# Attention and expert kernel on one core: k's second half prepared in round 0, q's copies behind round 0, the first pair's later loads behind round 4

## The chip, the cores and the metric

One core of a Trainium2 chip runs the program. The metric is the device time of one execution in microseconds (us). The engines have short names: PE is TensorE (matrix products and transposes), DVE is VectorE, ACT is ScalarE, POOL is GpSimd, and SP is SyncE, which here only issues transfers and passes semaphores. SPq in a row is SP's instruction queue. PEld is the weight load that belongs to a product on PE.

## The reference

Attention over pooled queries, whose output feeds four experts, weighted by the gate:

```python
q_pool = q.reshape(B, H, S // 2, 2, D).mean(axis=3)      # B=2, H=8, S=1152, D=64
scores = scale * np.matmul(q_pool, k.transpose(0, 1, 3, 2))
attn = np.exp(scores - np.max(scores, axis=-1, keepdims=True))
attn = attn / (np.sum(attn, axis=-1, keepdims=True) + 1e-09)
x = np.matmul(attn, v)  # then transposed to [B*S/2, H*D] = [1152, 512]
for e in range(4):
    h = np.maximum(x @ w1[e], 0.0)                       # w1[e]: [512, 1024]
    out += p[:, e:e + 1] * (h @ w2[e])                   # w2[e]: [1024, 512]
```

Everything is float32. The kernel writes each operand as a high part and a low part and adds three products of them.

## The kernel before

The attention comes first, then the experts. The change touches the attention alone. Heads are taken two at a time: eight pairs, `n` = 0 to 7, nine score tiles of 128 pooled queries by 1152 keys in each pair.

The loop over `n` runs five **rounds**, `round_(n, 0)` to `round_(n, 4)`. A round transposes two finished tiles (round 3: one), which is line 207 on PE with operand `sx`, makes the scores of tiles three places ahead (lines 384 and 392), and adds a part of the product with v (`PV_part`, line 478). DVE takes the minima of the scores (`neg_scores`, 444), ACT the exponentials (450), and both copy transposes out of PSUM (340, 342). The scores run ahead, so that round 4 of pair n already makes the scores of pair n+1. At its end a round may prepare **items**: `item_q` and `item_k` transpose pieces of the coming pair's q and k on PE, ACT copies them to `raw`, and POOL splits them into a high and a low part (`pool_split`, 214 and 215). `KTS` gives three pieces of k: 0 is key tile 8 and travels with `item_q`, 1 is tiles 0 to 3, and 2 is tiles 4 to 7, k's second half.

POOL's results still lie in the wrong rows. `stack_k` (285) copies k from `kab` to `k2` on chip, two transfers of 64 rows. `move_q` (293) copies a half `y` of q from the staging area `stq` to `q2`, two transfers; a pair needs four. `load_q` (170) and `load_kv` (174) fetch from memory. All of these are issued by SP, in program order.

One more thing stands in SP's queue. From pair 1 on, the scores of two tiles share a PSUM bank, and `S_rows` orders them by a **relay**: SP's `nop` at line 402 waits for a product on PE (tile f+1's columns), and PE's first product of tile f's last 128 columns waits for the relay:

```python
mm = [S_term(s, t2, 1, j) for j in range(3)][-1]
relay = nc.sync.nop()
tc.add_manual_dep(relay.ins, mm.ins.name, SYNC, reason="row tiles of one bank")
```

There is one relay in each of the rounds 0, 1, 2 and 4. What SP has in front of a relay must be issued before the relay can pass; and a transfer that waits, or that takes long to issue, holds the relay and PE behind it.

Of the kernel before, what the change touches and what calls it, by code (L numbers as in the profile page):

```python
# [17 lines left out]
def attention_moe_kernel(ctx, tc, q, k, v, probs, w1, w2, out):  # L18
    nc = tc.nc
# [3 lines left out]
    P = 128  # L23
# [23 lines left out]
    xr = const.tile([P, NKT, NT], F32, name="xr")  # L47
# [6 lines left out]
    kn = kq[:, :2 * KT * D].rearrange("p (h t d) -> p h t d", h=2, t=KT)  # L54
# [44 lines left out]
    WCH = [(0, 2), (2, 4), (4, 6), (6, 7)]  # L99
# [48 lines left out]
    with ExitStack() as actx:  # L148
# [18 lines left out]
        def load_q(n, t0=0, t1=9):  # L167
            b, hp = pairs[n]
            src = q[b, 2 * hp:2 * hp + 2].rearrange("h (p t r) d -> (h p) t r d", p=HALF, t=9)
            nc.sync.dma_start(qn[:, t0:t1], src[:, t0:t1])  # L170

        def load_kv(dst, src, n, h0=0, h1=2):
            b, hp = pairs[n]
            nc.sync.dma_start(
                dst[:, h0:h1], src[b, 2 * hp + h0:2 * hp + h1].rearrange("h (p t) d -> p h t d", p=P))
# [106 lines left out]
        def stack_k(n, t0, t1):  # L282
            cols = slice(t0 * P, t1 * P)
            for h in range(2):
                nc.sync.dma_start(  # L285
                    k2[n % 2][ROWS[1 - h], :, cols].bitcast(F32), kab[n % 2][ROWS[h], :, cols].bitcast(F32))

        def move_q(n, y):
            for half in range(2):
                r = slice(half * HALF, (half + 1) * HALF)  # L290
                dst = q2[n % 2].rearrange("p z s (y x) -> p (z s) y x", y=2)[r, :, y, :]
                st = stq.rearrange("p z s j x -> p (z s) (j x)")[y * HALF:(y + 1) * HALF]
                nc.sync.dma_start(dst.bitcast(F32), st.bitcast(F32))  # L293
# [33 lines left out]
        def item_r(n, grp, eng):  # L327
            r = rs[n % 2][:, 4 * grp:]

            def use(pt):  # L330
                copy(eng, halves(rb[grp], 0, 2), pt[:, :, :2])
                if grp:
                    for a, h in enumerate(ROWS):
                        copy(eng, rb[1][h, 256:], pt[h, a, 2])
            return [spread[:, j * P:(j + 1) * P] for j in range(2)] + (
                [r[:, 4:5].to_broadcast([P, P])] if grp else []), use
# [145 lines left out]
        def inv_sums(n, grp):  # L482
            c0, c1 = ((0, 4), (4, 9))[grp]
            r = rs[n % 2][:, c0:c1]
            nc.vector.tensor_scalar_add(r, sums[n % 2][:, c0:c1], 1e-9)
            nc.vector.reciprocal(r, r)
            nc.vector.tensor_copy(
                spread.rearrange("p (c x) -> p c x", x=HALF), r[:, :4].unsqueeze(2).to_broadcast([P, 4, HALF]))
# [113 lines left out]
        def load_probs():  # L602
            for hh in range(2):
                nc.sync.dma_start(
                    pr.rearrange("p (b t) e -> p b t e", b=2)[hh * HALF:(hh + 1) * HALF],
                    probs.rearrange("(b p t) e -> p b t e", b=2, p=HALF))

        def gate_weights():
            nc.vector.tensor_reduce(prs, pr, AX.X, ALU.add)
            nc.vector.tensor_scalar_add(prs, prs, 1e-9)  # L610
            nc.vector.reciprocal(prs, prs)
            nc.gpsimd.tensor_tensor(pr, pr, prs.unsqueeze(2).to_broadcast([P, 18, E]), ALU.mult)
            for a in range(2):
                sl = slice(a * HALF, (a + 1) * HALF)
                nc.gpsimd.tensor_copy(pw[sl], pr[sl, a:a + 17:2, :])
# [5 lines left out]
        def round_(n, r, items=(), spare=(), beside=(), wide=False, before=None, mid=None, ahead=False, heads=both, swap=True):  # L621
            ts_ = [g for g in ((9 * n + 5,) if r == 3 else [9 * n + (-1, 1, 3, 0, 6)[r] + j for j in range(2)]) if g >= 0]
            x, count, side = ts_[0], len(ts_), first[0]
            f = x + 3
            transposed([(x, 0, 8)], tp, heads)
            if before:
                before()
            rest = scores(f, count, side, wide)
            transposed([(x, 8, 9)] + [(g, 0, 1) for g in ts_[1:]], tp, both[:1], beside)
            for g in pending:  # L630
                exps(g)
            pending.clear()
            neg_scores(f)

            def prepared():
                if spare:
                    prepare(spare, tp)
                if items:
                    prepare(items, SIDE[side if count == 2 else 1 - side])

            if count == 2:
                scores2(f + 1, rest)
                transposed([(ts_[1], 1, 9)], tp, both)
                exps(f)
                if ahead:
                    prepared()
                neg_scores(f + 1)
            pending.append(f + count - 1)
            if mid:
                mid()  # L650
            pn, grp, k0, k1 = ((n - 1, 1, 0, 5), (n - 1, 1, 5, 9), (n, 0, 0, 3), (n, 0, 3, 6), (n, 0, 6, 9))[r]
            if pn >= 0:
                PV_part(pn, grp, k0, k1)
                if k1 == KT:
                    finish(pn, grp)
            if not ahead:
                prepared()
            if items and count == 2 and swap:
                first[0] = 1 - side
            while behind:  # L660
                behind.pop(0)()

        for n in range(NP):
            last = n == NP - 1
            two = n + 2 < NP

            if n == 0:
                round_(0, 0, [item_k(1, 1, nc.scalar), item_k(1, 2, nc.scalar)], wide=True)
            elif n == 1:
                round_(1, 0, [item_r(0, 1, nc.vector), item_k(2, 1, nc.scalar)], [item_k(2, 2, nc.scalar)],  # L670
                       before=lambda: inv_sums(0, 1))
            else:
                round_(n, 0, [item_r(n - 1, 1, nc.vector)], before=lambda: inv_sums(n - 1, 1))
            if n and two:
                load_q(n + 2)
                load_kv(kn, k, n + 2)
            if n > 1 and not last:
                move_q(n + 1, 0)
            if last:
                split_x("S3", 1, slice(0, HT), xr[:, 1, :HT], nc.gpsimd)  # L680
                load_w2(0)
                w1_hi(0, WCH[:1])
                w1_lo(0, WCH[:1])


            if n == 0:
                round_(0, 1, [item_q(1, nc.vector)], wide=True, before=lambda: add_q(nc.vector), ahead=True, swap=False)
                load_q(2)
                load_kv(kn, k, 2)
                load_kv(vn[1], v, 1)  # L690
                load_probs()
            elif n == 1:
                round_(1, 1, [item_q(2, nc.scalar)])
                stack_k(2, 0, 9)
            elif last:
                round_(n, 1)
                w1_hi(0, WCH[1:2])
                w1_lo(0, WCH[1:2])
            else:
                round_(n, 1, [item_k(n + 1, 2, nc.scalar)])  # L700
                stack_k(n + 1, 0, 9)
                move_q(n + 1, 1)


            round_(n, 2, [item_r(n, 0, nc.vector)], before=lambda: inv_sums(n, 0),
                   heads=both if n else both[:1] * 2, swap=n > 0)
            if n == 0:
                split_q2m(1, rawq(1))
            if n == 1:
                move_q(2, 0)  # L710
                move_q(2, 1)
            if n and two:
                add_q(nc.gpsimd)
                join_k(0)
                join_k(1)
            if n == NP - 2:
                load_w1(0)
            if last:
                w1_hi(0, WCH[2:])
                w1_lo(0, WCH[2:])  # L720
                load_w1(1)


            round_(n, 3, [item_q(n + 2, nc.scalar)] if n and two else [])
            if n and not last:
                load_kv(vn[(n + 1) % 2], v, n + 1)
            if n == 0:
                add_q(nc.gpsimd)
                join_k(0)
                join_k(1)  # L730
                join_k(2, xr[:, 1, :4 * P])
            if last:
                break


            round_(n, 4, [item_k(n + 2, 1, nc.scalar)] if n and two else [])
            if n == 1:
                gate_weights()
            if n == NP - 2:
                w1_sums(0)  # L740
# [188 lines left out]
```

## Time and profile before

| | |
|---|---|
| median of 3 runs | 679.97 us (678.71 to 680.31) |
| the profiled execution's own time | 681.35 us |
| its span, first to last instruction | 679.5 us |
| mean granted clock of TensorE | 0.952 |
| PE busy in the span | 624.0 us (92%) |
| DVE, ACT, POOL busy | 381.9, 297.4, 340.0 us |

The span is the time between the first and the last instruction of the profiled execution; 1.85 us of its own time lie around it. Attention takes the first 300 us or so. In rows of a timeline the columns are: start in us, duration in us, engine, line, operation, what is written from what, sizes, and how many instructions are merged; in square brackets stands how long the engine had been idle, and what ended that.

### The profile page before, as it was taken

Reading aid. Unit: us, or ns where it says so; the run is one execution under the profiler, and the core shown is the slowest. Engines: PE = TensorE matmul, PEld = TensorE weight load, DVE = VectorE, ACT = ScalarE, POOL = GpSimd, SP = SyncE. Lnnn points to the kernel's source line nnn. Section 1 sums busy time; section 2 is a strip of 40 time slices with the busy share of each in tenths; the row PEclk is TensorE's granted clock in tenths of the full one; section 3 lists DMA queues with packets and bytes.
Section 4 is the critical chain, followed back from the end, with each engine's and each line's share of the span. In section 5 each row is a group of like instructions: output and inputs, shape, how many; then the busy total and the mean of one; then the engine's idle time right before and its main releaser. Section 6 shows DMA issues by size and latency. Waiting matters only on the chain.

```text
span 679.5 us, 12422 instructions
## 1 busy us (share of the span) xinstructions
PE 624.0 (92%) x5045; PEld 523.8 (77%) x5045; DVE 381.9 (56%) x583; ACT 297.4 (44%) x545; POOL 340.0 (50%) x392
## 2 busy tenths in 40 slices
PE   8897959596887959979999999999999999999997
PEld 7665747384665747749889989988998899899886
DVE  6855747566583838666454445445444544544454
ACT  5754736364564727726244234423422441343130
POOL 4435434334142315857685467447645854674240
PEclk9987988989796969979999999999999999999999
DMA  4964652625445160111121111112120210210005
GB/s 149 211 194 90 161 121 59 143 72 139 98 111 127 34 167 32 33 31 42 53 63 32 40 53 49 46 32 62 32 63 32 62 32 32 62 34 28 32 1 139
DMA packets 38584, 50.90 MB, mean 75 GB/s; under 512 B 3072, under 2 KB 27008, under 8 KB 37632
## 3 DMA queue, kind: packets, MB, share of 16 engines
q1 hardware_dynamic: 37648, 48.94, 27.5%
q10 hardware_dynamic: 880, 1.18, 0.5%
q8 instruction: 39, 0.64, 0.4%
q14 instruction: 17, 0.14, 0.1%
HBM read 30.97 MB, written 2.36 MB: 49 GB/s over the span
## 4 chain that ended last, share of the span: by engine, by line
PE 86%; SPq 5%; DVE 3%; POOL 3%; issue 1%; ACT 1%; DMA 1%; DVEq 0%; ACTq 0%; POOLq 0%
PE banks L885 29%; PE banks L137 26%; PE banks L478 11%; PE banks L207 8%; PE banks L392 8%; SPq L293 3%; PE banks L384 3%; POOL kk L215 1%; SPq L285 1%; DMA kq<-in_k_dram 1%; DVE sx L444 1%; ACT raw L340 1%; POOL kk L214 1%; DVE q2all L546 0%; DVE aT L342 0%
## 5 line engine op out<-in xcount | busy, mean ns | idle before, releaser
L885 PE MATMUL banks<-w2s,hb 128*128 128x512 f32 (+1 forms) x876 | 199.3, 387 | 0.0
L885 PEld LDWEIGHTS banks<-w2s,hb 128*128 128x128 f32 x876 | 162.5, 188 | 32.7
L889 DVE SCALAR_TENSOR_TENSOR acc<-banks,pw,acc 128x512 f32<-128x512 f32 (+1 forms) x137 | 101.8, 743 | 81.0 <-PE banks L885 80.9
L444 DVE TENSOR_SCALAR_CACHE_REDUCE sx<-banks 128x1152 f32<-128x1152 f32 x72 | 97.3, 1351 | 63.4 <-PE banks L207 61.6
L118 POOL TENSOR_TENSOR kk<-kq,kk 128x512 fp32r<-128x512 f32 x64 | 72.2, 1160 | 116.1 <-ACT kk L110 116.1
L392 PE MATMUL banks<-kk,q2all 64*128 64x512 f32 (+1 forms) x504 | 75.9, 400 | 42.4 <-SPq L402 41.1
L340 ACT ACTIVATE aT<-banks 128x128 f32<-128x128 f32 (+1 forms) x145 | 59.9, 437 | 107.2 <-PE banks L207 106.2
L392 PEld LDWEIGHTS banks<-kk,q2all 64*128 64x128 f32 x504 | 56.4, 203 | 47.8 <-SPq L402 44.1
L450 ACT ACTIVATE sx<-sx,mn 128x1152 f32<-128x1152 f32 x72 | 90.4, 1256 | 2.5 <-DVE sx L444 2.5
L478 PE MATMUL banks<-aT,vn 128*64 128x320 f32 (+1 forms) x576 | 87.0, 446 | 0.0
L805 POOL TENSOR_TENSOR hb<-xr,hb 128x576 fp32r<-128x576 f32 x48 | 68.9, 1441 | 21.3 <-ACT hb L804 21.3
L137 PE MATMUL banks<-xb,kk 128*128 128x288 f32 x480 | 77.6, 298 | 0.0
L207 PE MATMUL banks<-ident,sx 64*128 64x64 f32 x1296 | 75.1, 238 | 1.0 <-ACT aT L340 0.5
L137 PE MATMUL banks<-q2all,kk 128*128 128x288 f32 x448 | 75.1, 296 | 0.0
L852 ACT ACTIVATE xr<-banks 128x576 f32<-128x576 f32 x14 | 9.1, 650 | 147.4 <-PE banks L137 147.4
L207 PEld LDWEIGHTS banks<-ident,sx 64*128 64x128 f32 x1296 | 61.2, 148 | 12.3 <-ACT aT L340 6.5
L137 PEld LDWEIGHTS banks<-xb,kk 128*128 128x128 f32 x480 | 69.0, 190 | 1.2 <-issue 1.0
L137 PEld LDWEIGHTS banks<-q2all,kk 128*128 128x128 f32 x448 | 64.6, 188 | 0.0
L478 PEld LDWEIGHTS banks<-aT,vn 128*64 128x64 f32 x576 | 40.8, 148 | 27.4 <-issue 5.3
L342 DVE COPY aT<-banks 128x512 f32<-128x512 f32 x71 | 48.9, 689 | 23.2 <-PE banks L207 22.6
L801 DVE TENSOR_TENSOR xr<-banks,xr 128x576 f32<-128x576 f32 x48 | 36.4, 758 | 40.4 <-PE banks L137 40.1
L137 PE MATMUL banks<-xa,kk 128*128 128x288 f32 x384 | 56.7, 296 | 0.0
(108 smaller groups left out, 636.8 us busy)
## 6 DMA issues: line engine op xcount, KB each, us to landing
kq<-in_moe_w_dram SPq DMA_DIRECT2D x64, 128.0 KB, 2.4
qsf<-in_moe_w_dram SPq DMA_DIRECT2D x16, 512.0 KB, 3.5
kk<-kk SPq DMA_DIRECT2D x14, 576.0 KB, 6.0
q2all<-q2all SPq DMA_DIRECT2D x28, 256.0 KB, 7.8
vn<-in_v_dram SPq DMA_DIRECT2D x8, 576.0 KB, 6.2
kq<-in_k_dram SPq DMA_DIRECT2D x7, 576.0 KB, 6.4
kq<-in_q_dram SPq DMA_DIRECT2D x7, 576.0 KB, 4.1
kk<-kk SPq DMA_DIRECT2D x4, 288.0 KB, 7.0
```

The lines of the kernel that those rows point to most:

```text
L118: nc.gpsimd.tensor_tensor(flat(w1s[u % 2][:, 1, a:b]), flat(wf[:, a:b]), flat(w1s[u % 2][:, 0, a:b].bitcast(F32)), ALU.subtract)
L137: nc.tensor.matmul(chain[:, c, :CW], w1s[u % 2][:, a, WI[wo], kt, :], xop(xo, z, kt)[:, c * CW:(c + 1) * CW], start=(first and kt == 0 and ...
L207: nc.tensor.transpose(pt[:, a, j, :], src[r], ident[r, r])
L340: nc.scalar.activation(dst, src, AF.Copy)
L342: nc.vector.tensor_copy(dst, src)
L392: return nc.tensor.matmul(dst, q2[n % 2][ROWS[a], zq, h, t * P:(t + 1) * P], src[n % 2][ROWS[a], zk, cs], start=(j == 0), stop=(j == 2), s ...
L444: nc.vector.tensor_scalar(sx[g % 3].rearrange("p (c x) -> p c x", c=c), view, -INV, None, ALU.mult, ALU.min, accum_out=mn[g % 3])
L450: nc.scalar.activation(sx[g % 3], sx[g % 3], AF.Exp, bias=mn[g % 3], scale=-1.0, accum_out=sums[n % 2][:, i:i + 1])
L478: nc.tensor.matmul(po[h * HALF:(h + 1) * HALF, :w], vn[n % 2][:, h, kt, :], aT[grp][:, h, kt, :], start=(kt == 0), stop=(kt == KT - 1))
L805: nc.gpsimd.tensor_tensor(lo, c, hi.bitcast(F32), ALU.subtract)
L885: nc.tensor.matmul(pc, h[:, a, sl, ts_], w[:, b, sl, c0:c1], start=(m == 0), stop=(m == len(ops) - 1))
L889: nc.vector.scalar_tensor_tensor(ac, pc, pw[:, tt, e:e + 1], ac, ALU.mult, ALU.add)
```

## The change

In pairs 2 to 6, `item_k(n + 1, 2)` moves from round 1 into round 0, all four copies of `move_q` stand directly behind round 0 and ahead of the loads, and `stack_k` stays behind round 1 alone. In pair 1 `stack_k` is cut in two: key tiles 0 to 7 behind round 1, and tile 8, which comes with `item_q`, behind round 2. In pair 0 the loads of pair 2's q and k, of pair 1's v and of the gate, with POOL's work on them, move from behind rounds 1 and 3 into round 4, behind its second set of scores and so behind its relay. No arithmetic is added or removed; two small transfers are added by the cut.

```diff
+        def later_loads():
+            load_q(2)
+            load_kv(kn, k, 2)
+            load_kv(vn[1], v, 1)
+            load_probs()
+            add_q(nc.gpsimd)
+            join_k(0)
+            join_k(1)
+            join_k(2, xr[:, 1, :4 * P])
...
-                round_(n, 0, [item_r(n - 1, 1, nc.vector)], before=lambda: inv_sums(n - 1, 1))
+                round_(n, 0, [item_r(n - 1, 1, nc.vector)] + ([] if last else [item_k(n + 1, 2, nc.scalar)]),
+                       before=lambda: inv_sums(n - 1, 1))
+                if not last:
+                    move_q(n + 1, 0)
+                    move_q(n + 1, 1)
             if n and two:
                 load_q(n + 2)
                 load_kv(kn, k, n + 2)
-            if n > 1 and not last:
-                move_q(n + 1, 0)
...
-                load_q(2)
-                load_kv(kn, k, 2)
-                load_kv(vn[1], v, 1)
-                load_probs()
-            elif n == 1:
-                round_(1, 1, [item_q(2, nc.scalar)])
-                stack_k(2, 0, 9)
-            elif last:
-                round_(n, 1)
-                w1_hi(0, WCH[1:2])
-                w1_lo(0, WCH[1:2])
             else:
-                round_(n, 1, [item_k(n + 1, 2, nc.scalar)])
-                stack_k(n + 1, 0, 9)
-                move_q(n + 1, 1)
+                round_(n, 1, [item_q(2, nc.scalar)] if n == 1 else [])
+                if last:
+                    w1_hi(0, WCH[1:2])
+                    w1_lo(0, WCH[1:2])
+                else:
+                    stack_k(n + 1, 0, 9 if n > 1 else 8)
...
             if n == 1:
+                stack_k(2, 8, 9)
                 move_q(2, 0)
                 move_q(2, 1)
...
-            if n == 0:
-                add_q(nc.gpsimd)
-                join_k(0)
-                join_k(1)
-                join_k(2, xr[:, 1, :4 * P])
...
-            round_(n, 4, [item_k(n + 2, 1, nc.scalar)] if n and two else [])
+            round_(n, 4, [item_k(n + 2, 1, nc.scalar)] if n and two else [], mid=None if n else later_loads)
```

In SP's queue, from pair 1's `stack_k` to pair 2's loads and copies, the transfers stand as follows (+ now, - before; the relays are no transfers and have no rows: in pair 2, one stands ahead of the first loads or copies, one ahead of `stack_k`, and one ahead of the load of v):

```order
-L285 DMA kk_74<-kk_74 64x2304 x2
+L285 DMA kk_74<-kk_74 64x2x1024 x2
+L285 DMA kk_74<-kk_74 64x2x128 x2
 L293 DMA q2all<-q2all 64x4x256 x4
 L174 DMA vn_84<-in_v_dram 128x2x576
+L293 DMA q2all<-q2all 64x4x256 x4
 L170 DMA kq<-in_q_dram 128x1152
 L174 DMA kq<-in_k_dram 128x2x576
-L293 DMA q2all<-q2all 64x4x256 x2
 L285 DMA kk_75<-kk_75 64x2304 x2
-L293 DMA q2all<-q2all 64x4x256 x2
 L174 DMA vn_85<-in_v_dram 128x2x576
```

Pair 1's stack became four transfers, and in pair 2 (as in 3 to 6) two copies of q left the place behind the stack and all four stand ahead of the loads.

On PE, the transposes of k's second half (operand `qsf`) in pair 2 stand behind round 0's items instead of behind round 1's product with v:

```order
 L207 MATMUL banks<-ident,spread 128x64 x4
 L207 MATMUL banks<-ident,rs_101 128x64 x2
+L207 MATMUL banks<-ident,qsf 128x64 x8
 L207 MATMUL banks<-ident,sx_87 128x64 x16
 L392 MATMUL banks<-kk_74,q2all 128x512 x3
```

```order
 L207 MATMUL banks<-ident,sx_88 128x64 x16
 L478 MATMUL banks<-aT_90,vn_85 64x320 x8
-L207 MATMUL banks<-ident,qsf 128x64 x8
 L207 MATMUL banks<-ident,sx_86 128x64 x16
 L392 MATMUL banks<-kk_74,q2all 128x512 x3
```

Eight transposes moved one round ahead, and nothing else changed its place on PE.

## Rows read from the trace of the kernel before

**Rows 1.** The waits by pair of engines: us in total, times, longest us

```profile
PE banks L392 <- SPq L402: 41.1, 7, 7.3
```

**Rows 2.** The timeline of SP in pair 3

```profile
116.18 0.35 SPq L170 DMA_DIRECT2D kq<-in_q_dram  x1
116.63 0.37 SPq L174 DMA_DIRECT2D kq<-in_k_dram  x1
117.06 1.26 SPq L293 DMA_DIRECT2D q2all<-q2all  x2
129.90 1.47 SPq L285 DMA_DIRECT2D kk<-kk  x2
131.43 4.46 SPq L293 DMA_DIRECT2D q2all<-q2all  x2
```

**Rows 3.** The timeline of PE in pair 3, and the start of pair 4

```profile
121.54 1.40 PE L392 MATMUL banks<-kk,q2all 64*128 64x512 f32 x12
...
127.43 1.28 PE L392 MATMUL banks<-kk,q2all 64*128 64x512 f32 x9
136.00 0.47 PE L392 MATMUL banks<-kk,q2all 64*128 64x128 f32 x1 [7.29 <-SPq L402]
...
145.20 0.53 PE L207 MATMUL banks<-ident,qsf 64*128 64x64 f32 x10
...
145.63 0.66 PE L207 MATMUL banks<-ident,sx 64*128 64x64 f32 x16
...
150.28 0.46 PE L207 MATMUL banks<-ident,qsf 64*128 64x64 f32 x8
150.58 0.66 PE L207 MATMUL banks<-ident,sx 64*128 64x64 f32 x16
```

**Rows 4.** The timeline of POOL in pair 3

```profile
128.61 1.26 POOL L215 TENSOR_TENSOR kk<-raw,kk 128x512 fp32r<-128x512 f32 x1
...
131.24 1.26 POOL L185 TENSOR_TENSOR qsf<-kq 128x512 f32<-128x512 f32 x1
```

**Rows 5.** Stretches: busy us of engines (instructions), granted clock, DMA share, GB/s

```profile
116.18:152.01 35.83, 28.54 (x357) 21.43 (x354) 23.12 (x40) 19.89 (x40) 12.86 (x21) 0.90 0.47 114
...
124.00:125.00 1.00, 1.00 (x20) 0.68 (x18) 1.00 (x3) 1.00 (x3) 0.00 (x0) 1.00 0.12 26
...
133.00:134.00 1.00, 0.00 (x0) 0.00 (x0) 0.00 (x0) 0.00 (x0) 0.94 (x3) 0.50 0.81 147
```

**Rows 6.** The timeline of PE in pair 7, which prepares no later pair

```profile
260.87 0.71 PE L207 MATMUL banks<-ident,sx 64*128 64x64 f32 x16
...
272.84 0.71 PE L207 MATMUL banks<-ident,sx 64*128 64x64 f32 x16
...
279.40 1.95 PE L384 MATMUL banks<-kk,q2all 128*128 128x512 f32 x9 [0.56 <-DVE sx L444]
...
282.94 0.71 PE L207 MATMUL banks<-ident,sx 64*128 64x64 f32 x16
```

**Rows 7.** The timeline of PE in pair 1, and the start of pair 2

```profile
41.80 0.71 PE L207 MATMUL banks<-ident,sx 64*128 64x64 f32 x16
...
55.12 0.66 PE L207 MATMUL banks<-ident,sx 64*128 64x64 f32 x16
...
61.12 0.47 PE L392 MATMUL banks<-kk,q2all 64*128 64x128 f32 x1 [4.25 <-SPq L402]
...
77.16 0.66 PE L207 MATMUL banks<-ident,sx 64*128 64x64 f32 x16
```

**Rows 8.** The timeline of SP in pairs 0 and 1

```profile
32.32 0.83 SPq L170 DMA_DIRECT2D kq<-in_q_dram  x1
33.19 1.47 SPq L174 DMA_DIRECT2D kq<-in_k_dram  x1
...
61.13 7.12 SPq L293 DMA_DIRECT2D q2all<-q2all  x4
```

**Rows 9.** The timeline of PE in round 4 of pair 0

```profile
37.00 0.32 PE L392 MATMUL banks<-kk,q2all 64*128 64x128 f32 x1 [0.35 <-SPq L402]
```

**Rows 10.** Transfers, the page's last part: count, KB each, median us to landing

```profile
q2all<-q2all SPq DMA_DIRECT2D x28, 256.0 KB, 7.8
```

## The prediction

> **What bounds the kernel now.** I read the page first: PE is busy 92% of the span, so what can be gained is the time in which PE waits, or runs at the lower clock. The list of waits says where. One row of it has 41.1 us, seven times: PE's products of line 392 wait for SP's relay [rows 1]. No other wait of PE in that list is near it in size. Seven times is once for each of the pairs 0 to 6.
>
> Then the timelines of one pair. In pair 3 PE issues the nine products that don't need the relay at 127.43, ends them at 128.71, and goes on at 136.00 after 7.29 us of nothing [rows 3]. SP's queue shows why the relay is late. POOL ends the low part of k's second half at 129.87 [rows 4]; only then does SP issue the stack, at 129.90, for 1.47 us, and behind it two copies of q that take 4.46 us to issue, until 135.89 [rows 2]. The relay of round 2 stands behind these. So the wait is POOL's lateness (128.7 to 129.9), then 1.5, then 4.5 us of issuing. The second cost is the clock: at 133 us the granted clock is 0.50, the lower level of 1.2 GHz, after PE had been idle since 128.7 [rows 5], and PE goes on at that level.
>
> The same two copies of q cost 1.26 us when they are issued behind loads and not behind a stack [rows 2]. So a copy takes long to issue where copies on the chip are still under way in front of it.
>
> **The change, part by part.** I sum against the profiled execution (681.35 us, span 679.5). Its rounds are dated by the 16 transposes that open each.
>
> *Pairs 2 to 6, the wait and the clock.* Pair 2 opens at 77.16 [rows 7] and pair 7 at 260.87 [rows 6]: 183.71 us for five pairs, 36.7 each. What would a pair take whose round 2 does not wait? Pair 7 shows it: it prepares nothing, has no transfer that waits ahead of its relays, and needs 282.94 - 260.87 = 22.07 us for rounds 0 to 3 [rows 6]. To this come round 4 with its eight transposes of k, 150.58 - 145.63 = 4.95 us [rows 3]; `item_q`'s twelve transposes in round 3, 145.63 - 145.20 = 0.43 us [rows 3]; and the eight of k's second half, now in round 0, 150.58 - 150.28 = 0.30 us [rows 3]. That is 27.75 us. Pair 6 has neither `item_q` nor the piece of k in round 4, 0.73 us less, 27.0. Five pairs: 4 x 27.75 + 27.0 = 138.0 us, a gain of 45.7 us. It splits into 5 x 7.3 = 36.5 us of waits [rows 1] and 9.2 us, 1.8 a pair, of clock. Pair 7's 0.56 us in which PE waits for DVE [rows 6] is kept in: DVE then has no pause any more in which to catch up. If it stays hidden, 2.8 us more are gained.
>
> *The moved item.* Its instructions are the same eight transposes, one copy on ACT and two splits on POOL. PE pays 0.30 us in round 0 and saves it in round 1. POOL is busy 12.86 us of 35.83 [rows 5] and has nothing else at that place, so its split ends well before round 1 does. It is late only if ACT is; ACT has 19.89 us of work in the pair [rows 5].
>
> *SP ahead of round 1's relay.* This is the new risk. Four copies and two loads now stand between the relay of round 0 and that of round 1. In pair 3 SP was free at 116.18 [rows 2]. The relay of round 1 is wanted when its nine products end: 121.54 + 1.28 = 122.82 [rows 3], plus 0.30 for the moved transposes, 123.1. So SP has 6.9 us. Cheapest, from rows: 2 x 1.26 + 0.35 + 0.37 = 3.2 us [rows 2], no wait. Dearest: four copies behind a stack took 7.12 us and two loads behind copies 0.83 + 1.47 us [rows 8], 9.4 us, a wait of 2.5 us. The copies now start with an empty queue, so at least the first two cost 0.63 us each. I take 0.5 us for each of the pairs 2 to 5 (pair 6 has no loads), 2.0 us; with the clock's 1.8 us on top, the dear end is 4 x 4.3 = 17 us.
>
> The Trainium skill, "DMA: Bandwidth & Descriptors", section "Issuing engines are not separate DMA queues", says that the time a sequencer takes to start a transfer is usually small beside the transfer itself. The trace agrees for copies behind loads and disagrees for copies behind a stack [rows 2]; by the page this term would be nothing and the time 2 us lower.
>
> *The stack behind round 1.* It no longer waits for POOL. Issued near 124, it has 5 us until round 2's relay. In the trace the loads and two copies issued from 116.18 on are off the queues in the stretch from 124 to 125, where the DMA share is 0.12 [rows 5]; with two copies more that is 127 or so, so that the stack may be held, but ends before the relay is wanted near 129. I take nothing; if it is held by the 4.5 us of [rows 2], round 2 waits for about 1 us.
>
> *The loads, 3 to 6 us later.* POOL wants the new q at 131.24 today [rows 4], some 7 us after the DMAs went quiet. Now the loads end near 127 and POOL is free for them near 129. Hidden; without that cover `item_q` of round 3, some 7 us behind, is the next to be late.
>
> *Pair 1.* It takes 77.16 - 41.80 = 35.36 us, with 4.25 us of wait and the low clock behind that [rows 7]. Now: rounds 0 and 1 as they are, 55.12 - 41.80 = 13.32 [rows 7]; rounds 2 and 3 as in pair 7, 282.94 - 272.84 = 10.10 [rows 6]; 0.43 and 4.95 as above: 28.80 us. But the four copies of q now follow only after POOL's last split, near 60, and the scores of round 4 want them near 66. They take 1.26 to 7.12 us to issue [rows 2, 8] and 7.8 us to land in the middle [rows 10], so PE waits between 0 and 5 us; I take 1.5 (the large stack is gone from in front of them). Gain: 5.1 us.
>
> *Pair 0.* The relay of round 4 waited 0.35 us [rows 9], behind loads that now come later. With some of the low clock behind it I take 1.0 us, between 0 and 2.
>
> The sum: 45.7 - 2.0 + 5.1 + 1.0 = 49.8 us. The profiled execution would take 631.6 us. The median lies 1.4 us under the profiled execution: 679.97 - 49.8 = 630.2, so 630.
>
> **The rivals.** *A, the forecast*, 630 us: nothing of size takes the place of round 2's relay. For it speaks pair 7, which runs all of its relays without a wait. *B, round 1's relay takes over*: the copies are slow even with an empty queue, and SP reaches the relay 2.5 us late, with the clock falling again. That gives back 17 - 2 = 15 us: 645. For it: 256 KB copies on chip were slow four times in a row [rows 8]. Against it: there a stack was ahead of them. *C, DVE becomes the bound*: it has 23.12 us of work per pair [rows 5], 83% of 27.75 us, and it has today a pause of 7 us in each pair. If the chain through DVE makes a pair 30 us, 2.3 us in five pairs: 641. Against it: pair 7 loses 0.56 us to DVE and no more. *D, slower*: if each copy were taken only when the one before had landed, four would hold SP for 4 x 7.8 = 31 us [rows 10]; round 1's relay would then be some 25 us late, a loss of 25 - 9.1 = 16 us a pair and 64 in four pairs, 694 us or above. It decides from 9.1 us of lateness, that is from 16 us of issuing. Two copies in 1.26 us [rows 2] speak against it. *E, the split does not come sooner*: ACT or POOL reach the moved item only a round later, and the stack waits as before. Then only the copies' 4.5 us are gone, with half the clock: 5 x 5 + 5 = 30 us, 650. POOL's idle time in that place speaks against it.
>
> **How the numbers follow.** A 0.62, B 0.17, C 0.12, E 0.06, D 0.03. The range goes from A's good end (no wait in round 1, none in pair 1, DVE hidden: 630 - 2 - 1.5 - 2.8 - 1: about 622) to B, with pair 1's dear end of 3.5 us (near 649): 622 to 649. About 0.3% is what a measurement of this kernel can tell from no change. A, B, C and E are all faster, 0.97, of which I keep 0.02 for no change and 0.01 more for slower, since several of them together eat most of the gain: 0.94, 0.02, 0.04.
>
> **What would show it.** The wait of line 392 for line 402 falls from 41 us to a few; pairs 2 to 6 open 27 to 28.5 us apart; the granted clock stays at 1.00 through rounds 2 and 3; the stack is issued within a microsecond of round 1's relay; the four copies behind round 0 take 2.5 to 5 us to issue. I am wrong if PE shows a new idle time in round 1 or, in round 4 of pair 1, one of more than 3 us, if DVE is over 90% busy with PE waiting for line 444, or if pairs stay above 30 us.

## The result, and the profile after

The changed kernel takes 628.42 us in the median of four runs (627.41 to 629.73), the kernel before, run beside it, 679.34 us (677.28 to 680.31). The ratio is 0.9255, with an interval of 0.9225 to 0.9286. The forecast was 630 us, the range 622 to 649. The profiled execution took 629.14 us (span 627.4, mean granted clock 0.991), against 681.35 us before (679.5, 0.952): 52.2 us less, where the sum said 49.8.

The page of the changed kernel, engines' busy time and the granted clock in 40 slices:

```profile
PE 607.0 (97%) x5045; PEld 511.6 (82%) x5045; DVE 378.5 (60%) x583; ACT 296.8 (47%) x545; POOL 340.5 (54%) x392
...
PEclk9989999999999997999999999999999999999999
```

PE does the same work and is busy 97% of the span instead of 92%. Its waits, us in total, times, longest us (the first four of the list):

```profile
PE banks L207 <- DVE spread L487: 4.2, 1, 4.2
PE banks L207 <- ACT aT L340: 3.3, 8, 1.0
PE banks L384 <- DVE sx L444: 3.3, 6, 0.6
PE banks L392 <- DMA q2all<-q2all: 1.4, 2, 0.8
```

The row that stood at the top before, 41.1 us of line 392 for the relay [rows 1], is gone: no relay of the program is waited for. The first row here is one wait at the attention's end, which was there before as well (4.5 us). The second and third are small waits that come back once in most pairs; they are read below.

SP in pair 4 of the changed kernel, which answers to pair 3 before [rows 2] (columns as in those rows):

```profile
128.75 3.64 SPq L293 DMA_DIRECT2D q2all<-q2all  x4
132.44 1.66 SPq L170 DMA_DIRECT2D kq<-in_q_dram  x1
134.19 0.68 SPq L174 DMA_DIRECT2D kq<-in_k_dram  x1
137.69 1.12 SPq L285 DMA_DIRECT2D kk<-kk  x2
```

PE in the same pair, from its opening to that of pair 5, which answers to [rows 3]:

```profile
127.32 0.66 PE L207 MATMUL banks<-ident,sx 64*128 64x64 f32 x16
...
134.35 1.41 PE L392 MATMUL banks<-kk,q2all 64*128 64x512 f32 x12
136.13 0.34 PE L207 MATMUL banks<-ident,sx 64*128 64x64 f32 x4 [0.37 <-ACT aT L340]
...
139.96 0.71 PE L207 MATMUL banks<-ident,sx 64*128 64x64 f32 x16
...
146.67 1.94 PE L384 MATMUL banks<-kk,q2all 128*128 128x512 f32 x9 [0.56 <-DVE sx L444]
...
155.56 0.66 PE L207 MATMUL banks<-ident,sx 64*128 64x64 f32 x16
```

SP is through with copies and loads at 134.87 and reaches round 1's relay there. PE ends the nine products that don't need it at about 134.35 + 1.28 = 135.63 (1.28 from [rows 3]). So the relay is 0.8 us early: nothing is lost, but the cover is thin. Read in the same way it is 1.9 us in pair 2, 0.5 in pair 3 and some 0.7 in pair 5. Round 2, whose wait of 7.29 us was the subject, opens at 139.96 and doesn't wait for its relay.

Two pairs as stretches (columns as in [rows 5]):

```profile
99.06:127.32 28.26, 27.14 (x360) 19.93 (x357) 23.23 (x40) 19.81 (x40) 12.97 (x20) 1.00 0.57 144
127.32:155.56 28.24, 27.04 (x359) 19.92 (x357) 23.23 (x40) 19.79 (x40) 12.99 (x20) 1.00 0.56 143
```

A pair took 35.8 us at a mean clock of 0.90 [rows 5]; it takes 28.25 at 1.00. By the 16 transposes that open each, pairs 2 to 6 take 29.42, 28.26, 28.24, 27.04 and 26.37 us, 139.33 in all, where they took 183.71 [rows 6, 7].

### The profile page after: what moved, and what is told of

Same layout as the page of the kernel before. It is cut to its first block, busy times and chain, and to the rows that moved or that the text cites. A ratio compares the mean times of both kernels' runs of the same rounds, so it can differ in the third digit from the quotient of the medians.

```text
span 627.4 us, 12421 instructions
## 1 busy us (share of the span) xinstructions
PE 607.0 (97%) x5045; PEld 511.6 (82%) x5045; DVE 378.5 (60%) x583; ACT 296.8 (47%) x545; POOL 340.5 (54%) x392
## 3 DMA queue, kind: packets, MB, share of 16 engines
HBM read 30.97 MB, written 2.36 MB: 53 GB/s over the span
## 4 chain that ended last, share of the span: by engine, by line
PE 84%; DVE 6%; DMA 3%; POOL 3%; issue 1%; ACT 1%; SPq 1%; DVEq 0%; ACTq 0%; POOLq 0%
PE banks L885 31%; PE banks L137 28%; PE banks L478 10%; PE banks L207 6%; PE banks L392 6%; DMA q2all<-q2all 2%; PE banks L384 2%; DVE sx L444 1%; DMA kq<-in_k_dram 1%; POOL q2all L215 1%; DVE aT L342 1%; ACT raw L340 1%; DVE spread L487 1%; DVE rb L342 1%; POOL q2all L214 1%
## 5 line engine op out<-in xcount | busy, mean ns | idle before, releaser
L444 DVE TENSOR_SCALAR_CACHE_REDUCE sx<-banks 128x1152 f32<-128x1152 f32 x72 | 97.2, 1350 | 25.9 <-PE banks L207 24.1
L478 PE MATMUL banks<-aT,vn 128*64 128x320 f32 (+1 forms) x576 | 80.6, 420 | 0.0
L207 PE MATMUL banks<-ident,sx 64*128 64x64 f32 x1296 | 66.7, 229 | 4.6 <-ACT aT L340 3.3
L207 PEld LDWEIGHTS banks<-ident,sx 64*128 64x128 f32 x1296 | 54.0, 140 | 20.4 <-ACT aT L340 11.6
L392 PE MATMUL banks<-kk,q2all 64*128 64x512 f32 (+1 forms) x504 | 66.3, 377 | 1.4 <-DMA q2all<-q2all 1.4
L478 PEld LDWEIGHTS banks<-aT,vn 128*64 128x64 f32 x576 | 38.4, 139 | 24.7 <-issue 1.5
L137 PEld LDWEIGHTS banks<-xa,kk 128*128 128x128 f32 x384 | 53.7, 188 | 1.2
```

The costliest lines, as they stand in the source:

```text
L137: nc.tensor.matmul(chain[:, c, :CW], w1s[u % 2][:, a, WI[wo], kt, :], xop(xo, z, kt)[:, c * CW:(c + 1) * CW], start=(first and kt == 0 and ...
L207: nc.tensor.transpose(pt[:, a, j, :], src[r], ident[r, r])
L392: return nc.tensor.matmul(dst, q2[n % 2][ROWS[a], zq, h, t * P:(t + 1) * P], src[n % 2][ROWS[a], zk, cs], start=(j == 0), stop=(j == 2), s ...
L444: nc.vector.tensor_scalar(sx[g % 3].rearrange("p (c x) -> p c x", c=c), view, -INV, None, ALU.mult, ALU.min, accum_out=mn[g % 3])
L478: nc.tensor.matmul(po[h * HALF:(h + 1) * HALF, :w], vn[n % 2][:, h, kt, :], aT[grp][:, h, kt, :], start=(kt == 0), stop=(kt == KT - 1))
```

## The experiments

Ratios are against the kernel before, run beside them. Its medians were 678.41 us for the parts alone, 678.70 for `busy`, `copies_twice`, `loads_first` and `k_before_r`, 678.41 for `spread_act` and `spread_act_k`, and 680.32 for the last two.

### Each part alone

`k_only`: k's item in round 0, with one half of q's copies still behind the stack.

```diff
-                round_(n, 0, [item_r(n - 1, 1, nc.vector)], before=lambda: inv_sums(n - 1, 1))
+                round_(n, 0, [item_r(n - 1, 1, nc.vector)] + ([] if last else [item_k(n + 1, 2, nc.scalar)]),
+                       before=lambda: inv_sums(n - 1, 1))
...
-                round_(n, 1, [item_k(n + 1, 2, nc.scalar)])
+                round_(n, 1, [item_q(2, nc.scalar)] if n == 1 else [])
```

> The kernel before, with one part of the change alone: in pairs 2 to 6 the item of k's second half is prepared in round 0, so that the stack behind round 1 no longer waits for POOL. The copies of q stay where they were, two behind the loads and two behind the stack. Theory 1 (the two causes add up: POOL's lateness with the stack's issue, some 2.7 us, and the copies' issue, 4.5 us): the stack is issued 2 us after round 1's relay, with 1.1 us, the copies behind it take 4.5 us, and the relay of round 2 comes some 2 us late instead of 7.3: gain 5 x 5 = 25 us of waits, and most of the clock's 9 us if a wait of 2 us does not lower it: 650 us, 645 to 660. Rival 2 (the copies are slow because of the DMA traffic, not because of the place: with the stack earlier, they meet the loads under way and take 2 x 4 us): the wait stays near 5 us, 665 to 670.

652.98 us, ratio 0.9619 (0.9591 to 0.9647). SP in pair 3, and one of PE's waits in round 2:

```profile
117.78 1.47 SPq L285 DMA_DIRECT2D kk<-kk  x2
119.31 4.78 SPq L293 DMA_DIRECT2D q2all<-q2all  x2
```

```profile
124.21 0.32 PE L392 MATMUL banks<-kk,q2all 64*128 64x128 f32 x1 [2.36 <-SPq L402]
```

The stack still follows POOL's split, but the split is done at 117.76, 4.1 us before PE has ended the nine products that don't need the relay (121.85), so that POOL no longer makes the relay late. The two copies behind the stack still take 4.78 us, and the relay behind those is 2.36 us late.

`q_only`: all four copies behind round 0, k's item in round 1 as before.

```diff
                 round_(n, 0, [item_r(n - 1, 1, nc.vector)], before=lambda: inv_sums(n - 1, 1))
+                if not last:
+                    move_q(n + 1, 0)
+                    move_q(n + 1, 1)
...
-            if n > 1 and not last:
-                move_q(n + 1, 0)
...
-                move_q(n + 1, 1)
```

> The kernel before, with the other part alone: in pairs 2 to 6 all four copies of q are issued behind round 0, ahead of the loads. K's second half stays in round 1, and the stack behind it still waits for POOL. Theory 1: round 2's relay waits for POOL's 1.2 us and the stack's 1.1 to 1.5 us only, 2.7 us instead of 7.3: gain 5 x 4.6 = 23 us of waits, and part of the clock's 9 us: 652 us, 645 to 660. Rival 2 (the copies only move the hold-up to the relay of round 1): a new wait of 2 us or more in round 1, gain under 15 us, 665 or above.

652.24 us, ratio 0.9606 (0.9571 to 0.964). SP in pair 3, and PE in its round 2:

```profile
108.20 3.66 SPq L293 DMA_DIRECT2D q2all<-q2all  x4
...
122.26 1.12 SPq L285 DMA_DIRECT2D kk<-kk  x2
```

```profile
123.49 0.47 PE L392 MATMUL banks<-kk,q2all 64*128 64x128 f32 x1 [2.43 <-SPq L402]
```

Here the stack is what is late: it is issued at 122.26, when POOL's split has ended (122.23). This is rival E's case, the copies gone from behind the stack and the split no sooner, for which the prediction had 650 us. Of the wait of 7.3 us `k_only` leaves 2.0 to 2.4 in a pair and `q_only` 2.4 to 2.5, and they gain 25.4 and 26.2 us, a little more than half of what both gain together (below). Neither is enough by itself, because the relay stands behind both.

What is left of the wait still lowers the clock in pairs 3 to 6. The stretch behind it in pair 3, of `k_only` and then of `q_only`:

```profile
124.21:130.00 5.79, 5.79 (x62) 4.65 (x63) 3.75 (x7) 3.63 (x8) 0.78 (x2) 0.71 0.81 200
```

```profile
123.49:130.00 6.51, 6.51 (x49) 4.73 (x51) 3.33 (x5) 3.51 (x7) 2.81 (x6) 0.50 0.94 216
```

Over pairs 2 to 6 the mean granted clock was 0.87 before; it is 0.95 with either part and 1.00 in the changed kernel.

`pairs26` has both parts and leaves pairs 0 and 1 as before; `first_pairs` has only what the change does in pairs 0 and 1.

```diff
# first_pairs, against the kernel before
-            round_(n, 4, [item_k(n + 2, 1, nc.scalar)] if n and two else [])
+            round_(n, 4, [item_k(n + 2, 1, nc.scalar)] if n and two else [], mid=None if n else later_loads)
...
-                stack_k(2, 0, 9)
+                stack_k(2, 0, 8)
...
             if n == 1:
+                stack_k(2, 8, 9)
                 move_q(2, 0)
```

> Both parts in pairs 2 to 6, with pairs 0 and 1 as in the kernel before. By the sum of the prediction the gain of these five pairs is 45.7 - 2.0 us; the trace of the changed kernel has the five pairs at about 43 us less. Expected 636 us, 633 to 639. If the two parts alone gain 25 and 23 us, they add up or fall short by little; if one alone had gained nearly all, this would be no better than that one.

> Only the changes of pairs 0 and 1: pair 0's later loads in round 4 behind its relay, pair 1's stack cut in two. Pairs 2 to 6 as in the kernel before. In the trace of the changed kernel pair 1 is 6.6 us and pair 0 0.7 us shorter: expected 672 us, 670 to 674. Rival (pair 1's four copies, now behind POOL's last split, hold up round 4): gain of 3 us or less, 677.

634.14 us, ratio 0.9344 (0.931 to 0.9378), and 673.52 us, ratio 0.9919 (0.9892 to 0.9947). PE's waits for the relay, of `pairs26` and then of `first_pairs`:

```profile
PE banks L392 <- SPq L402: 4.4, 2, 4.3
```

```profile
PE banks L392 <- SPq L402: 36.5, 5, 7.4
```

The 4.3 us are pair 1's, the 36.5 those of pairs 2 to 6; each kernel takes away its own. Gains of 44.3 and 4.9 us make 49.2, and the whole change gained 50.9, so the two places add within what the intervals allow. No run takes pairs 0 and 1 apart. The two parts in pairs 2 to 6 don't add: 25.4 + 26.2 is 51.6, 7.3 more than 44.3. Of 41.1 us of waits `k_only` leaves 14.6 and `q_only` 16.7, pair 1's 4.3 among them; in pairs 2 to 6 they take away 26 and 24 of 36.5 us. Each alone takes away more than half of one and the same wait, and with both, SP is through before PE asks, so that the surplus is worth nothing. Of the waits that surplus is some 14 us; of the time it is only 7.3. That fits the clock, which comes back in full only with both: in the profiled executions pairs 2 to 6 shrink by 2.0 us more than their waits in `k_only`, by 4.2 in `q_only` and by 7.9 in the changed kernel.

### The clock's share

`busy` is the kernel before with 60 products of 128 x 128 put into the wait, in round 2 of pairs 2 to 6, with a result that nothing reads. The relay comes as late as before, but PE is not idle.

```diff
+            if tiles[f][1] == 6 and 2 <= tiles[f][0] <= 6:
+                for _ in range(NBUSY):
+                    nc.tensor.matmul(PVB[:, :P], identr, identr, start=True, stop=True, skip_group_check=True)
```

> The kernel before with 60 products of 128x128 more on PE in round 2 of pairs 2 to 6, between the nine products that don't need the relay and the first that does; their results go to a bank that is free there and are not used. They fill the wait for the relay (7.3 us) with work, without changing any transfer. Theory (the wait also costs by the lower clock behind it, 1.8 us a pair): the granted clock stays at 1.00 behind the relay and the kernel gains about 9 us, 671 us, 668 to 673. Rival (what the rounds behind the wait lose is not the clock but the start of DVE and ACT from rest): no gain, 679 us; if the products take longer than the wait, slower.

668.47 us, ratio 0.9849 (0.9825 to 0.9873). PE in pair 3, and the stretch around the wait and that behind it:

```profile
126.29 6.92 PE L410 MATMUL banks<-identr 128*128 128x128 f32 x60
133.51 0.32 PE L393 MATMUL banks<-kk,q2all 64*128 64x128 f32 x1 [0.30 <-SPq L403]
```

```profile
128.00:136.00 8.00, 7.70 (x82) 7.10 (x83) 1.76 (x3) 1.75 (x5) 3.54 (x7) 1.00 0.90 192
136.00:141.00 5.00, 5.00 (x53) 3.46 (x49) 3.58 (x6) 3.42 (x6) 0.00 (x0) 1.00 0.60 160
```

The granted clock is 1.00 through the wait and behind it. Before, it was 0.50 in the wait [rows 5], and behind it:

```profile
136.00:141.00 5.00, 5.00 (x43) 3.99 (x45) 2.85 (x4) 3.27 (x6) 0.00 (x0) 0.63 0.91 214
```

That alone is worth 10.2 us, 2.0 a pair: the loss by the lower clock, with the wait itself left as it was. DVE and ACT still rest through most of the wait (1.76 and 1.75 us busy of 8.00), so their start from rest, the rival, isn't what was lost. The prediction had 9.2.

### How thin the new place is

`copies_twice` issues each of the four copies behind round 0 twice; `loads_first` puts the two loads ahead of the four copies.

```diff
# copies_twice, against the changed kernel
-                    move_q(n + 1, 0)
-                    move_q(n + 1, 1)
+                    for _ in range(2):
+                        move_q(n + 1, 0)
+                        move_q(n + 1, 1)
# loads_first, against the changed kernel
-                if not last:
-                    move_q(n + 1, 0)
-                    move_q(n + 1, 1)
             if n and two:
                 load_q(n + 2)
                 load_kv(kn, k, n + 2)
+            if n > 1 and not last:
+                move_q(n + 1, 0)
+                move_q(n + 1, 1)
```

> The changed kernel with every copy of q in pairs 2 to 6 issued twice (the second writes the same data again): eight copies and two loads between the relays of round 0 and round 1. SP reached round 1's relay 0.8 us before PE wanted it in the changed kernel. Theory (the new place is hidden by less than a microsecond, and more issuing there becomes a wait): four more copies at about 1.4 us, 5.6 us; PE waits about 4.8 us in round 1 of pairs 2 to 5 and 2 us in pair 6, with some clock behind it: 628 + 21 to 628 + 32, 650 to 660. Rival (issuing is cheap with the stack gone from in front: the copies take 0.6 us each): 2.4 us more, a wait of 1.6 us at most, 636 or less.

> The changed kernel with the two loads ahead of the four copies of q in pairs 2 to 5. Theory (a copy is slow to issue only with copies on chip under way in front of it; behind loads it takes 0.63 us): SP reaches round 1's relay after some 3.3 to 4.5 us instead of 5.9 us, and the time stays the same, 628 us within 0.3%, as nothing waited there. Rival (what is under way in front counts, whatever it is: the third and fourth copy are held by the loads): 6 to 9 us, a wait of up to 2.5 us in round 1, 632 to 645.

With the copies doubled the kernel takes 651.78 us, ratio 0.9613 (0.9576 to 0.965), 23.4 us more than the changed kernel. SP in pair 4, and PE in round 1 of pairs 3 and 4:

```profile
136.99 9.28 SPq L293 DMA_DIRECT2D q2all<-q2all  x8
```

```profile
113.51 0.47 PE L392 MATMUL banks<-kk,q2all 64*128 64x128 f32 x1 [4.28 <-SPq L402]
...
148.00 0.47 PE L392 MATMUL banks<-kk,q2all 64*128 64x128 f32 x1 [4.13 <-SPq L402]
```

The two loads behind the copies end at 147.89, so that SP is held for 10.9 us instead of 6.1. These 4.8 us, less the 0.8 that were to spare, are 4.0; PE waits 4.13 in pair 4, and 2.24, 4.28, 3.53 and 1.48 us in pairs 2, 3, 5 and 6, 15.7 in all. Rival B is a real mechanism, and in pairs 3 to 5 the changed kernel stands less than a microsecond away from it.

With the loads first it is 627.76 us, ratio 0.9249 (0.9229 to 0.9269), no change that can be measured. SP in pair 4:

```profile
128.53 0.34 SPq L170 DMA_DIRECT2D kq<-in_q_dram  x1
128.98 0.37 SPq L174 DMA_DIRECT2D kq<-in_k_dram  x1
129.40 4.47 SPq L293 DMA_DIRECT2D q2all<-q2all  x4
```

SP is held from 128.53 to 133.87, 5.3 us where it was 6.1 in the changed kernel, since a load ahead of the copies takes 0.35 us to issue and one behind them 0.7 to 1.7. That is cover, not time. The 5.3 us are more than the 3.3 to 4.5 that were expected: the third and fourth copy were slow to issue behind loads too, 1.43 and 1.55 us.

### The small waits that are left

Two theories for the rest. One: each small wait of PE can be had back by itself. The other: PE then meets the next thing, on another engine. In round 1 of the changed kernel PE waits 0.37 us for ACT. The timelines of ACT and DVE in pair 4 show why:

```profile
134.09 0.79 DVE L342 COPY rb<-banks 128x256 f32<-128x256 f32 x3 [0.39 <-PE banks L207]
```

```profile
134.99 0.60 ACT L340 ACTIVATE raw<-banks 128x512 f32<-128x512 f32 x1 [1.73 <-DVE rb L342]
135.48 0.59 ACT L340 ACTIVATE aT<-banks 128x512 f32<-128x512 f32 x1
```

ACT's copy of the moved item waits 1.73 us for DVE's copies of the item ahead of it, and the copy that PE needs stands behind it. `k_before_r` puts k's item ahead of the other:

```diff
-                round_(n, 0, [item_r(n - 1, 1, nc.vector)] + ([] if last else [item_k(n + 1, 2, nc.scalar)]),
+                round_(n, 0, ([] if last else [item_k(n + 1, 2, nc.scalar)]) + [item_r(n - 1, 1, nc.vector)],
```

> The changed kernel with the two items of round 0 in the other order in pairs 2 to 6: k's second half ahead of the sums' rows. In the changed kernel ACT's copy of k waits until DVE has copied the sums' rows, 1.7 us in pair 4, and PE then waits 0.37 us for ACT. Theory (the two copies exclude each other, whichever is first; ACT is free earlier, so that it should go first): PE's wait of 0.3 to 0.4 us in round 1 goes, gain 1 to 2 us, 627 us. Rival (DVE then waits for ACT and is late with its own copies): same or up to 2 us slower.

629.7 us, ratio 0.9275 (0.9249 to 0.93): the same. PE's waits have changed their engine: those for ACT fall from 3.3 to 1.5 us, and those for line 342 of DVE rise from 0.8 us to

```profile
PE banks L207 <- DVE aT L342: 3.7, 9, 0.8
```

`spread_act` goes for the 0.56 us of line 444, by giving DVE's copy that spreads the inverse sums (line 487) to ACT; `spread_act_k` does both.

```diff
-            nc.vector.tensor_copy(
-                spread.rearrange("p (c x) -> p c x", x=HALF), r[:, :4].unsqueeze(2).to_broadcast([P, 4, HALF]))
+            nc.scalar.activation(
+                spread.rearrange("p (c x) -> p c x", x=HALF), r[:, :4].unsqueeze(2).to_broadcast([P, 4, HALF]), AF.Copy)
```

> The changed kernel with one DVE instruction of rounds 0 and 2 of each pair, the copy that spreads the inverse sums (1.1 to 1.2 us, ahead of a round's first minima), given to ACT, which waits there for PE and has room (19.8 us of 28.2). Theory (what is left on PE's path behind round 0 and 2 is the chain through DVE, 0.76 us in rounds 2 to 3 and 0.37 us in round 1 of each pair): these waits shrink, 3 to 7 us less, 622 to 626 us. Rival (ACT's copy waits for DVE's reciprocal and pushes the exponentials back by 0.6 us; PE then waits for ACT): same within 0.3% or slower.

> As the run before, with the items of round 0 in the other order as well (k's second half first). With DVE free 1.2 us sooner, DVE's copies of the sums' rows are no longer what ACT waits for, so the order should matter less than it did: within 1 us of the run before. Rival (the two copies still exclude each other on their bank, and DVE's late start is now after ACT's): 1 to 3 us slower or faster than the run before.

629.15 us, ratio 0.9277 (0.9249 to 0.9305), and 627.92 us, ratio 0.9266 (0.9239 to 0.9294): both the same as the changed kernel, where 622 to 626 were expected. In `spread_act` the waits for line 444 fall from 3.3 to 0.8 us, and pair 3 takes 27.8 us instead of 28.3; pairs 5 and 6, which had no such wait, take 0.2 and 0.55 us more. What pairs 2 to 7 gain, 1.9 us, went in pair 1. PE there, and two stretches around it:

```profile
66.44 1.40 PE L392 MATMUL banks<-kk,q2all 64*128 64x512 f32 x10 [1.07 <-DMA q2all<-q2all]
```

```profile
66.00:68.00 2.00, 1.56 (x16) 1.53 (x18) 0.00 (x0) 0.00 (x0) 0.00 (x0) 0.86 1.02 239
68.00:70.00 2.00, 2.00 (x23) 1.96 (x21) 1.37 (x2) 1.66 (x4) 0.92 (x2) 0.50 0.75 240
```

PE finds q's copies not landed, waits 1.07 us, and the granted clock falls to 0.50: pair 2 opens at 72.38 instead of 69.64. The expectation of the next run puts this down to rounds 2 and 3, which are 0.8 us shorter. But rounds 0 and 1 are 0.5 us longer, and the rows show that the copies came later. SP in the changed kernel, then in `spread_act`:

```profile
60.26 3.64 SPq L293 DMA_DIRECT2D q2all<-q2all  x4
```

```profile
61.49 3.63 SPq L293 DMA_DIRECT2D q2all<-q2all  x4
```

Pair 1 opens at 40.89 and at 40.79, and PE is at round 4's products of line 392 after 24.2 and 24.1 us. The copies start 19.4 and 20.7 us into the pair: POOL's last split is 0.4 us later, and the second transfer of the small stack in front took 1.51 us to issue instead of 0.61. So the last two kernels send pair 1's copies of q ahead of the small stack: `spread_q1` from `spread_act`, `spread_k_q1` from `spread_act_k`.

```diff
             if n == 1:
-                stack_k(2, 8, 9)
                 move_q(2, 0)
                 move_q(2, 1)
+                stack_k(2, 8, 9)
```

> The run spread_act, and in pair 1 the four copies of q ahead of the small stack of key tile 8. In spread_act rounds 2 and 3 of pair 1 are 0.8 us shorter, the copies have not landed when round 4 wants them, PE waits 1.07 us there and goes on at a granted clock of 0.50. Theory (that is where the gain of the five later pairs went, 0.45 us each): the copies need only POOL's first split, 2.3 us sooner, so they land in time, the wait and the low clock go, and the time is 625 us, 623 to 626.5. Rival (the small stack, now behind the copies, comes too late for round 4 instead): 628 or above.

> The run before with k's second half first among round 0's items. In spread_act_k the wait for the copies in pair 1 was 0.76 us and the later pairs were 28.0 us apart, 27.8 without the change of order. Expected: within 1 us of the run before; if the order matters at all, 1 us slower.

626.53 us, ratio 0.9212 (0.9188 to 0.9235), and 626.67 us, ratio 0.9208 (0.9178 to 0.9238). PE in pair 1 of `spread_q1`, with round 4's scores and the opening of pair 2:

```profile
62.86 1.40 PE L392 MATMUL banks<-kk,q2all 64*128 64x512 f32 x12
...
67.34 0.66 PE L207 MATMUL banks<-ident,sx 64*128 64x64 f32 x16
```

The wait is gone: pair 1, from 39.06 on, takes 28.28 us instead of the changed kernel's 28.75, and pair 2 28.07 instead of 29.42. The order of the items again made no difference. The ratios are 0.4 to 0.5% better than the changed kernel's 0.9255, but the intervals still touch (0.9225 to 0.9286), and each is against other runs of the kernel before. It is a tendency and not a result; 625 us was expected of `spread_q1`.

## Why the prediction was right

**Pairs 2 to 6.** The sum had 138.0 us for the five, with 2.0 for SP in round 1: 140.0. They take 139.33. The split was right as well: the waits on the relay went, and `busy` shows 10.2 us of clock where 9.2 were put down. The template from pair 7 and rounds of before, 138.0, held to one percent, but partly by two errors against each other; that 140.0 comes nearer still is luck, as its 2.0 us for SP didn't come. Pairs 3 and 4 are 0.5 us longer than 27.75 (28.26 and 28.24), and have the small wait for ACT in round 1 that the prediction did not see; pair 2 is 29.42, with a wait for ACT of 0.97 us in round 0 besides. Pairs 5 and 6 are 27.04 and 26.37, 0.6 to 0.7 us shorter than their templates, for the most part since the 0.56 us for DVE that was kept in for all five did not come in those two.

**SP ahead of round 1's relay.** Taken at 2.0 us, it cost nothing. The issuing was sized well: copies and loads hold SP from 128.75 to 134.87, 6.1 us, between the ends of 3.2 and 9.4 and inside the budget of 6.9. But the step that explained the size fell in part. It said that a copy takes long where copies are still under way in front of it, and that loads are cheap company. In pair 4 the four copies took 0.62, 0.61, 0.80 and 1.36 us, with an empty queue in front; with two loads in front they took 0.63, 0.61, 1.43 and 1.55. The first two go at once in both, and the later ones are held. The 1.26 us of [rows 2] were two copies that happened to be the first two. The place of a copy in its row counts as well, and the price of four is 3.6 to 4.5 us, not twice 1.26.

The Trainium skill, "DMA: Bandwidth & Descriptors", section "Issuing engines are not separate DMA queues", has the start of a transfer as usually small beside the transfer, and by it this term was nothing. The term was nothing, but not for that reason: copies and loads hold SP for 6.1 us, and PE's other work covers them.

**The stack behind round 1.** The prediction said that it no longer waits for POOL, and "within a microsecond of round 1's relay". It still waits for POOL, and is issued at 137.69, 2.8 us after SP reached that relay, since ACT's late copy made POOL late. POOL in pair 4:

```profile
135.67 0.62 POOL L214 TENSOR_SCALAR kk<-raw 128x512 fp32r<-128x512 f32 x1 [4.05 <-ACT raw L340]
136.37 1.29 POOL L215 TENSOR_TENSOR kk<-raw,kk 128x512 fp32r<-128x512 f32 x1
```

The split ends at 137.66 and the stack follows at once. "It is late only if ACT is" was the right condition, and it came true; it costs nothing, because round 2 opens only at 139.96. Rival E was this at full size.

**Pair 1.** Predicted 28.80 + 1.5 us, it takes 69.64 - 40.89 = 28.75. The 1.5 us for q's copies did not come. They were issued in 3.64 us and landed after 3.5 to 4.5 us, not 7.8 [rows 10]. But nothing was to spare: the second of them is issued at 60.91 and lands 4.1 us later, at 65.0, and PE's products of line 392 begin at 65.07. That it just sufficed is luck: in `spread_act` the copies come 1.3 us later, and 1.07 us of wait appears. PE's 0.56 us for DVE ahead of round 4, which the sum had as well, is time that the copies could use, so the two terms may lie beside each other and not in a row; no run shows that by itself.

**Pair 0.** Round 4 takes 8.26 us instead of 8.98 (41.80 in [rows 7]): 0.7 us, for 1.0. One execution of each says little here: in `first_pairs`, `copies_twice`, `loads_first` and `k_before_r`, whose pair 0 is that of the changed kernel, it takes 6.3 to 8.2 us, and in `pairs26`, `k_only`, `q_only` and `busy`, with the pair 0 of before, 8.5 to 10.0.

**The rivals.** B did not happen, by 0.5 to 1.9 us in pairs 2 to 5; `copies_twice` shows it. C did not: DVE is busy 23.23 us in a pair of 28.24, 82%, and costs PE some 0.6 to 0.8 us in pairs 1 to 4 and in pair 7. D did not: the four copies were issued in 3.64 us, not one for each landing.

## What to carry to other kernels

Where an engine's queue passes a semaphore for another engine, every transfer in front of it is on that other engine's path with its issuing time, as soon as that engine has no other work to cover it, so the transfers are put where they can start at once, and as far as possible behind the relay. If a relay waits for two late things, the gains of mending each alone need not add: here each showed a little more than half, and their sum overstated the whole by 7.3 us. A stretch without the disease (here the last pair, which prepares nothing) is a good template for what remains; the small waits that it holds must be checked one by one, since some cover each other.

## What the runs showed of the hardware

**Copies on the chip, one behind the other.** In pairs 2 to 6 of the changed kernel and of `loads_first`, two of 256 KB are issued in 0.6 us each; the third and fourth of four take 0.6 to 2.1 us. In `copies_twice` the first six of eight take 0.61, 0.62, 0.80, 1.35, 1.23 and 1.15 us, and the last two, behind pauses of SP, 0.59 each. So a third copy soon after two others took 0.80 us or more, with nothing or with two loads ahead of them. In the changed kernel, where only pair 0's and pair 1's copies stand behind a stack, they land sooner than before (transfers: count, KB, median us to landing; 7.8 in [rows 10]):

```profile
q2all<-q2all SPq DMA_DIRECT2D x28, 256.0 KB, 4.6
```

**A copy on DVE that POOL holds up.** Pairs 5 and 6 have no wait of PE for line 444, and the timelines of DVE and POOL show what differs. In pair 4:

```profile
142.35 1.12 DVE L487 COPY spread<-rs 128x256 f32<-128x256 f32 x1
```

```profile
142.01 1.30 POOL L185 TENSOR_TENSOR qsf<-kq 128x512 f32<-128x512 f32 x1
```

In pair 6, where POOL does nothing at that time:

```profile
197.09 0.29 DVE L487 COPY spread<-rs 128x256 f32<-128x256 f32 x1
```

The same copy takes 1.12 us beside POOL's addition, and ends 0.16 us after it; alone it takes 0.29. In the changed kernel's attention, all 14 of these copies that found POOL at work end about 0.15 us after its instruction, in pair 5 after a short one (0.46 us), so that the copy takes 0.42. On ACT, in `spread_act`, it took 0.41 or 0.42 us each time, beside POOL or not. The Trainium skill, "SBUF — State Buffer", section "Who interferes with whom", says that some copies on DVE and any instruction of POOL exclude each other for an instruction's whole length, and that ACT waits for neither. The rows agree with that; no run took POOL's addition away alone, so it is read from rows and not shown by an experiment.

**The clock after a short wait.** In round 4 of pair 0, PE waits twice for q's copies, 0.66 and 0.77 us in the changed kernel, 0.41 and 0.78 us in `spread_q1`. The stretch from 37 to 39 us behind them, first of the changed kernel, then of `spread_q1`:

```profile
37.00:39.00 2.00, 2.00 (x23) 1.96 (x20) 1.35 (x2) 1.68 (x4) 0.00 (x0) 0.50 0.89 249
```

```profile
37.00:39.00 2.00, 2.00 (x30) 1.32 (x28) 1.98 (x4) 2.00 (x4) 0.00 (x0) 1.00 0.79 287
```

One is at the lower level, 1.2 GHz, the other at 2.4, and pair 1 opens at 40.89 and at 39.06. Some 0.25 us of wait stand beside a difference of 1.8 us. `spread_q1` differs in pair 0 by ACT's copy; `k_before_r`, whose pair 0 is that of the changed kernel, waits 0.22 and 0.74 us there and opens pair 1 at 39.13. In pair 2 of the changed kernel a wait of 0.97 us left the clock at 1.00. In `q_only` even 2.51 us in pair 2 did, with this stretch behind it, where 2.43 us in pair 3 were followed by 0.50:

```profile
93.76:99.00 5.24, 5.24 (x66) 4.00 (x67) 4.26 (x7) 4.00 (x8) 2.81 (x6) 1.00 0.95 210
```

The length of a short wait alone did not tell in these runs whether the clock falls.
